# New instruction lists for a fused attention and bilinear feed-forward kernel: the first weight block's first quarter is multiplied first, and 24 identity products stand ahead of it

## The chip, the core and the metric

The kernel runs on one core of one Trainium2 chip. The metric is device microseconds from the first to the last instruction as the runtime times them, lower is better. The core's engines each have a queue of their own that runs in program order: TensorE (PE), VectorE (DVE), ScalarE (ACT), GpSimd (POOL), and SyncE (SP), which here only issues DMA transfers.

## The reference

Eight batches of memory attention, and a feed-forward network with two linear factors on the result:

```python
a = np.exp(phi - phi.max(axis=2, keepdims=True))
a = a / (a.sum(axis=2, keepdims=True) + 1e-09)             # phi: 8 x 8 heads x 576 x 32
k_m = np.einsum('bhsm,bhsd->bhmd', a, k)
v_m = np.einsum('bhsm,bhsd->bhmd', a, v)
scores = (1.0 / np.sqrt(64)) * np.matmul(q, k_m.transpose(0, 1, 3, 2))
attn = softmax(scores)                                     # over 32 memories
x = heads_joined(np.matmul(attn, v_m))                     # 4608 x 512
return ((x @ w1) * (x @ w2) @ w3) @ w_out                  # w1, w2: 512 x 1024; w3: 1024 x 1024; w_out: 1024 x 512
```

The weights come as 64-bit floats, and everything is computed in 32-bit.

## The kernel before, in words

**Weights.** Each weight arrives in HBM as 64-bit words. A block of them is one task of five steps, `C1` to `C5` in the lists: sign (DVE, later ACT), high word (ACT), low word (ACT), shift (DVE), join (DVE). The first task is the first quarter of the first 128 rows of w3 (256 columns), the second is the first 128 rows of w_out, the third is the next quarter of w3's rows; then come further row blocks of w3 and w_out in turn. SP fetches the blocks into a ring of five buffers `raw`, and the last four blocks of w1 and w2 into buffers of the attention.

**The product of w3 and w_out** is made once, in 32-bit products of 128x512 (line 611; each leaves two records in the trace). `X0` and `X1` are the first two products and the next two of row block 0: `X0` needs the first and second task, `X1` the second and third. `W01` to `W07` are the other row blocks of w3's first half, four products each; `W100` to `W171` those of its second half, two products each. What comes out is copied and split into a high and a low part (`K`, `Kh`, `D`, `E`, `Dt`, `Et` and so on), the weight pieces.

**Attention of a batch** has the steps `bm` (PE, maximum spread), `bs` (DVE, maximum added), `be` (ACT, exponent), `mem` (PE, k_m and v_m, lines 254 and 263), `memc` (ACT), `block` (PE, transpose, line 285), `blockc` (ACT, lines 291 and 292, makes `km` and `vm`), `sc0` and `sc1` (PE, scores, line 303), `scc` (DVE, transposes, line 318), softmax steps, and at the end `tr`, `ah`, `al` and for all batches but the first `T1` to `T4`, `Th` and `Tl` (sums of the probabilities, split in high and low).

**Feed-forward of a batch.** `M0` to `M3` (PE, line 420) multiply v_m by w1 and w2. Batch 0 multiplies directly: `A01` is column quarter 0, product 1, and so on (line 718); `a` and `g` take each product out of PSUM on ACT and DVE. The later batches use seven block products `P` (line 748) for eight: `P60` is the sixth block product of quarter 0, which reads the probability sums `Th1` and `Tl1`. Seven products `O` (line 833) multiply the result by the weight pieces; `h` and `l` split their right sides into high and low. `C11` to `C22` copy and store.

**PSUM** has eight banks, kept as four slots on each of two sides; the class `Pair` takes one slot of each. A product waits until the slot that it was given has been read by everyone.

**The order** is written out by hand. Four lists of tokens, `FIRST` (batch 0), `SECOND`, `BATCH` (batches 2 to 6) and `LAST`, say in which order the steps are issued; each engine runs its own steps in that order. A token with "-" is a step of the same batch's attention, "+" of the batch after the next, without a sign of the next. A "!" puts an elementwise step on the other engine: splits and copies (`h`, `Kh`, `r`, `w`, `ah`, `Th`) go from ACT to POOL, differences and products (`l`, `al`, `T`, `Tl`, `v`, `Q`) from DVE to POOL, and `f`, `Sa`, `Sb`, `Sc` from POOL to DVE. Since the lists set which slot, buffer and queue place each step gets, they also set what it waits for.

Ahead of everything, `WARM` identity products of 128x128 run on PE (line 704).

Of the kernel before, what the change touches and what calls it, by code (L numbers as in the profile page):

```python
# [24 lines left out]
FIRST = """
C1 C2 C3 C1 C4 C5 C2 C3 C1 C4 C5 C2 C4 C3 C5 C1 C2 X1 C4 C3 C1 C2 C5 C4 C3 C5 C3 C1 C2 C4 C2 C5 C2 C1 C1 C3 C2 C4 C5
C4 phi0 C3 C1 C3 C4 C5 C1 C2 C3 X0 C5 C1 C2 C4 C5 W01 C3 C1 C4 C2 C3 C2 W02 W03 C4 C5 W04 C5 C1 C3 C1 C4 C5 C1 C2 W05
C4 C3 tok0 kv0 q0 C2 C3 C2 C5 C4 C5 -top -exp W06 -norm C1 C1 C2 C3 C2 C3 W07 -bm C4 C5 K2 Kh2 C4 C5 W101 C1 K3 Kt3
W100 K1 W111 -bs K0 C4 Kt0 Kl2 C3 Kh1 Kh0 W110 C2 r3 C4 -be -mem C5 C3 Kt2 r0 C1 -memc -block C5 -blockc -sc0 -sc1
-scc0 -scc1 Kt1 W121 W120 -mx0 C3 C2 -sb0 W130 -mx1 -ex0 C2 Kl0 -sb1 C3 W131 W141 C4 -sm0 W140 -ex1 C1 C5 C1 W150 W160  # L30
C2 C4 C4 C5 W151 r1! s0 -mu0 -tr0 C3 C2 C1 C1 C2 Kl1 -sm1 C4 C3 C1 W161 Kh3! s3 C4 s1 Kl3 -ah0! -mu1 C3 C5 C5 C2 -M0
-Mh0 -M1 C2 -al0 Q1! C5 W171 -Mh1 -Ml0 W170 A01 -tr1 -ah1! D2 -Ml1 A11 C3 Dt2 C4 Dt3 a01 Dt0 C1 g01 phi1 D3 a11 -al1!
C5 g11 C2 Et2 Et3 C4 A00 a00 g00 C1 -M2 -Mh2 E2 r2! s2 E3 A03 a03 -Ml2 g03 C3 C1 C3 C5 A12 Et0 A23 C4 F0 a12 g12 C5
Q2! A02 F2 t0 w0 tok1 a02 g02 D0 A10 a10 a23 top A13 D1 g23 bm z0 F3 g10 a13 g13 A20 exp bs Q0 a20 A22 g20 t3 be kv1
-M3 w2! y2 norm y0 q1 a22 w3 Dt1 mem E0 t2! z2 -Mh3 memc -Ml3 A32 z3 h10 f0! f1! block Q3 E1 g22 A33 f3! blockc sc0 F1
l10! a32 g32 a33 g33 Et1 h40 h41 scc0 mx0 y3 l41 f2! sc1 M0 Mh0 w1 A21 t1 A31 a31 Ml0 scc1 l40! Sa1! Mr0 a21 g21 mx1
Ms0 g31 A30 a30 g30 Sa3! sb1 z1 sb0 O40 O41 h11 O10 Sa0 h20 l11 O11 h60 Mt0 l20 Sb0 l60 Sc1! y1 Sb3! Sa2 p4 p1 O60
Sc0! O20 Mu0 M1 h21 l21 Sc2 h61 M2 l61 ex0 O21 sm0 O61 ex1 sm1 Sb1! Sb2! h70 l70! h71 mu1 Mr1 mu0 h50 l71 l50! u2 Ms1
C11 tr0 tr1 h51 l51 O70 O71 Mt1 ah0 al0 ah1 Mu1 h30 O50 al1 l30 Mh1 Sc3 h31 q2 T1 Mr2 T3! T2! l31 Ml1 O51 p5 Mh2 C21
O30 C22 T4! Th1 Tl1! O31 Th0 C12 Tl0! Ms2 Mt2! Mu2! Ml2  # L40
"""
SECOND = """
P10 P11 s00 s01 P60 P20 c10 P50 k200 k201 P70 k502 P30 v10 e402 e202 v20 P51 k512 P40 c30 v30 P31 phi1 s10 s11 tok1
h10! l10! P61 k210 P21 top k211 e212 c11 P71 bm v11 e412 exp P12 s20 s21 P41 f0 c31 P22 -M3 bs v21! v41 kv1 v31 be c12
mem -Mr3 norm f3 -Ms3 v12 v40 h11! l11! -Mt3! -Mu3! -Mh3 phi2 P62 memc block k220 k221 +top P52 k522 P72 -Ml3 e422 P32
e222 tok2 P13 blockc sc0 +exp scc0 sc1 scc1 s30 mx2 f2 s31 P42 c32 kv2 +bm v42! f1 P63 k230 k231 v32 P23 P53 k532 sb2
P73 v22! Sa0 P33 Sa1! e432 v43! e232 h60 l60! Sa3 P43 v23 ex2 +bs O10 h20 Sa2 l20 c33 v33 sm2 h70 O11 p1 O60 +be c13
v13 h21 +norm O20 +mem +memc Sb2! Sb1! l21 M0 h61! Sb0 l61 l70 Mr0 O61 Sc0! Mh0 Sb3! O21 h50 mu2 tr2 h71 u2 l71! h51
l51! O70 h41 Ml0 +block +blockc l50 Sc1! O71 O50 ah0 O51 al0 ah1 Ms0 l41 C11 al1! T1 h30 T3 h40 Sc3! l30 l40 M1 p5
Sc2! C22 Mt0 h31! l31! T2! Mh1 q2 Mu0 M2 Mh2 Mr1 Ms1 O30 Mt1 T4! Th0! Ml1 O40 Mu1 Th1 O41 C21 O31 Tl1! Tl0! C12 Mr2  # L50
Ms2 Mt2! Mu2! Ml2
"""
BATCH = """
phi2 P10 -M3 s00 s01 P20 c10 v10 P60 k200 k201 P50 P70 k502 P30 e402 v40! e202 -Mr3 -Ms3 v20! P11 P40 s10 s11 c30 v30
h10! -Mh3 P61 k210 k211 P51 +top -Ml3 -Mt3! P21 k512 P31 c11 e212 +exp -Mu3! P71 +bm P12 e412 P41 f0 v11 s20 s21 c31
P62 sc1 tok2 +bs l10! v31 sc0 v41 kv2 scc0 scc1 k220 h11! P22 P52 v21! c12 v12 mx2 P13 k522 k221 P32 e222 f3 P72 s30
+be P53 s31 P23 k532 P63 c13 e422 v42 k230 k231 v22 f1 l11! sb2 P33 e232 f2 P73 e432 v13 P42 Sa0 ex2 Sa1! P43 +mem v43
c32 v32 Sb0 h20 +norm sm2 +memc M0 Mr0 M2 Sa3 c33 v33 v23! M1 O10 Mh0 Ms0 Ml0 Sb3 O11 Sb1 h21 l21 h50 Sa2! l20! p1 l50
Sb2! h60 l60 O20 O21 Mh1 Sc1! h61 O60 C11 l61 O61 h51 h70 Mt0 Sc0! mu2 Mh2 u2 tr2 ah0 ah1 Sc2! l51! O50 Sc3! l70 h30
h71 l71! O51 p5 Mu0 O70 al0 l30 O30 Ml1 h40 l40 T1 h31 l31 Mr1 Ms1 O71 O31 h41! C22 O40 C12 +block q2 l41! Mt1 +blockc  # L60
T3! O41 Mu1 al1 T2 Th1 C21 Tl1 T4! Th0! Mr2 Tl0! Ms2 Mt2! Mu2! Ml2
"""
LAST = """
Mr1 P10 s00 s01 P11 +bm P20 P60 k200 Ml1 k201 P50 P70 c10 v10 k502 e402 P30 e202 Mr0 T1 +be P40 c30 v20! -M3 v40 s10
s11 P61 v30 h10 -Mh3 -Ml3 phi2 f0 sb2 l10! ah0 P51 k210 kv2 k211 P71 k512 e412 -Mr3 M2 Mu0! -Ms3 -Mt3 P31 e212 P21 tr2
sc1 Mt0 P12 s20 s21 scc1 Ms2 Mh0 v41! v21 P41 c31 v31 Mt2! +block f3! al1 q2 P22 c12 v12 P52 k522 +blockc c11 -Mu3!
P62 k220 k221 T2 P32 Mr2 e222 v11 P53 P72 f1! v22 k532 P13 e422 f2! v42 Sa0 Sa1 P33 +top h11 s30 s31 P63 k230 k231 Mh2
+norm e232 Mu2 P42 Th0! ah1! c32 v32 M1 P73 O10 h60 l60 mx2 T3 Ml0 e432 v43 Sb1 +mem Ms0 sm2 h20 l11! P23 Sb0! O11 p1
v23! Sa2! Tl0 +bs P43 Th1! l20 Sa3! h61 M0 Sb2! +exp O60 c13 v13 O20 l61! O61 h50 l50 Ms1 sc0 c33 v33 tok2 Sb3 h70 l70
h51 O50 l51 h40 h21 al0! l40 Mu1 u2 Sc0! l21 Ml2 Sc2! Sc1! O51 Mh1 p5 h71 Sc3! l71! O70 mu2 O21 C11 O71 C22 Tl1! ex2  # L70
O40 h30! l30! O30 h31 l31 h41! O31 T4! l41 C12 O41 C21 +memc scc0 Mt1!
"""
# [947 lines left out]
```

## Time and profile before

| | before |
|---|---|
| median of 3 runs | 496.7 us (496.6 to 497.26) |
| profiled execution, its own time | 498.98 us |
| its span, first to last instruction | 497.2 us |
| PE busy | 489.2 us (98%) |
| DVE busy | 430.1 us (86%) |
| ACT busy | 338.9 us (68%) |
| POOL busy | 265.2 us (53%) |
| mean granted TensorE clock | 0.997 |

A busy PE is one that has a product under way. The profile's page also cuts the span into slices and gives PE 9 tenths or more in all of them but the first and the last.

### The profile page before, as it was taken

What the parts mean: (1) busy time and instruction counts of PE and PEld (TensorE: products, weight loads), DVE (VectorE), ACT (ScalarE), POOL (GpSimd) and SP (SyncE); (2) the same over time, 40 slices, a digit from 0 to 9 for tenths busy, and PEclk for the clock granted to TensorE, in tenths of its full rate; (3) what the DMA queues carried; (4) which work ended last, traced back from release to release, by engine and by line L of the source; (5) the groups of instructions that cost most, each with busy time, mean ns of one, the idle gap of its engine ahead of it and who ended that gap; (6) DMA issues with size and microseconds to landing.
All of it is one profiled execution on the core that took longest, in us unless ns stands there. A gap on an engine that the chain in (4) does not pass through costs nothing.

```text
span 497.2 us, 11285 instructions
## 1 busy us (share of the span) xinstructions
PE 489.2 (98%) x4312; PEld 421.2 (85%) x4312; DVE 430.1 (86%) x812; ACT 338.9 (68%) x718; POOL 265.2 (53%) x256
## 2 busy tenths in 40 slices
...
GB/s 291 411 412 424 425 117 91 283 2 3 227 298 239 1 98 330 50 2 25 301 154 2 25 231 223 2 25 130 323 3 26 61 107 2 25 49 25 2 1 96
DMA packets 22390, 68.89 MB, mean 139 GB/s; under 512 B 1728, under 2 KB 9920, under 8 KB 20288
## 3 DMA queue, kind: packets, MB, share of 16 engines
...
## 4 chain that ended last, share of the span: by engine, by line
PE 97%; DMA 1%; ACT 0%; DVE 0%; SPq 0%; issue 0%; DVEq 0%
PE ps L833 36%; PE ps L748 32%; PE ps L611 12%; PE ps L420 6%; PE ps L718 5%; PE ps L254 3%; PE ps L303 2%; DMA raw<-in_w3T 1%; PE ps L263 1%; PE ps L285 0%; PE ps L232 0%; SPq L527 0%; DVE wo L599 0%; DVE w L599 0%; ACT w L584 0%
## 5 line engine op out<-in xcount | busy, mean ns | idle before, releaser
L833 PE MATMUL ps<-sh,Wh 128*128 128x288 f32 x448 | 132.8, 296 | 0.0
L833 PE MATMUL ps<-sh,Wl 128*128 128x288 f32 x448 | 132.2, 295 | 0.0
L833 PE MATMUL ps<-sl,Wh 128*128 128x288 f32 x448 | 132.0, 295 | 0.0
L818 POOL TENSOR_TENSOR sl<-g,sh 128x576 fp32r<-128x576 f32 x43 | 65.4, 1523 | 72.7 <-ACT sh L501 48.8
L833 PEld LDWEIGHTS ps<-sh,Wh 128*128 128x128 f32 x448 | 84.2, 188 | 6.8 <-ACT mh L431 5.0
L833 PEld LDWEIGHTS ps<-sh,Wl 128*128 128x128 f32 x448 | 84.2, 188 | 0.0
L833 PEld LDWEIGHTS ps<-sl,Wh 128*128 128x128 f32 x448 | 84.2, 188 | 0.0
L501 ACT CAST sh<-g 128x576 fp32r<-128x576 f32 x78 | 52.3, 684 | 24.3 <-PE ps L833 14.5
L611 PE MATMUL ps<-wo,w 128*128 128x512 f32 x128 | 57.5, 608 | 2.4 <-DVE w L599 2.4
L767 ACT COPY c<-ps 128x288 f32<-128x288 f32 x112 | 41.6, 412 | 18.9 <-PE ps L748 16.7
L773 DVE TENSOR_TENSOR c<-ps,c 128x288 f32<-128x288 f32 x112 | 44.8, 451 | 10.4 <-ACT c L767 8.4
L611 PEld LDWEIGHTS ps<-wo,w 128*128 128x128 f32 x128 | 24.6, 195 | 33.6 <-issue 29.3
L748 PE MATMUL ps<-sh,ms 128*128 128x288 f32 x224 | 51.8, 296 | 0.0
L728 ACT COPY a_sb<-ps 128x288 f32<-128x288 f32 x72 | 29.0, 406 | 22.7 <-PE ps L748 19.8
L818 DVE TENSOR_TENSOR sl<-g,sh 128x576 fp32r<-128x576 f32 x55 | 43.2, 792 | 0.7 <-ACT sh L501 0.4
L438 DVE TENSOR_TENSOR ml<-ps,mh 128x512 fp32r<-128x512 f32 x64 | 40.9, 681 | 1.3 <-ACT mh L431 1.2
L748 PEld LDWEIGHTS ps<-sh,ms 128*128 128x128 f32 x224 | 38.2, 188 | 1.0 <-ACT ps L761 0.8
L732 DVE TENSOR_TENSOR g<-ps,a_sb 128x288 f32<-128x288 f32 x72 | 32.0, 448 | 6.2 <-ACT a_sb L728 4.9
L456 DVE TENSOR_TENSOR tmp<-ps,tmp 128x256 f32<-128x256 f32 x84 | 32.8, 419 | 4.4 <-ACT mh L431 2.1
L431 ACT CAST mh<-ps 128x512 fp32r<-128x512 f32 x64 | 34.4, 596 | 2.2 <-PE ps L420 1.1
L748 PE MATMUL ps<-ah,mh 128*128 128x288 f32 x112 | 34.6, 309 | 0.0
L748 PE MATMUL ps<-sh,mh 128*128 128x288 f32 x112 | 33.2, 296 | 0.0
(151 smaller groups left out, 1280.4 us busy)
## 6 DMA issues: line engine op xcount, KB each, us to landing
...
q<-in_qT SPq DMA_DIRECT2D x8, 1152.0 KB, 5.9
...
```

What stands on the lines that cost most here:

```text
L420: nc.tensor.matmul(ps[t][g * M : (g + 1) * M], lhsT=vm[b % 2][d, g], rhs=w12_sb[q][d, :, g], start=True, stop=True,)
L431: nc.scalar.copy(out=mh[:, t], in_=ms["ps", q][t].rearrange("p (w f) -> p w f", w=2))
L438: nc.vector.tensor_tensor(out=ml[:, t], in0=x, in1=ms[q][0][:, t].bitcast(F32), op=ALU.subtract)
L456: nc.vector.tensor_tensor(out=tmp[:, j], in0=x, in1=tmp[:, y], op=op)
L501: nc.scalar.copy(out=out, in_=in_)
L611: nc.tensor.matmul(pw[r, i // 2][i % 2][:, cols], lhsT=x[:, i * P : (i + 1) * P], rhs=wos[k // half][:, k % half, cols], start=k == 0 and ...
L732: engine.tensor_tensor(out=G[n, f // half][:, f % half], in0=b, in1=a, op=ALU.mult)
L748: nc.tensor.matmul(G[bank, q][w][:, :HALF], lhsT=xs[x][:, w], rhs=ys[y], start=i in (1, 5) and k == 0, stop=i in (2, 3, 4) and k == 2, ski ...
L767: nc.scalar.copy(out=G["kept", i, q][:, j], in_=x)
L773: nc.vector.tensor_tensor(out=c, in0=x, in1=c, op=ALU.add)
L818: flexible().tensor_tensor(out=lo, in0=src, in1=hi.bitcast(F32), op=ALU.subtract)
L833: nc.tensor.matmul(ps[j][:, :HALF], lhsT=piece(x, s, 2 * part + k)[:, jc], rhs=y[:, k], start=i in first and part == 0 and k == 0 and t == ...
```

## The change

All four lists are new, `WARM` is 24 instead of 16, and `block_product` looks up the sums of the weights only for the products that use them, so that a list may name a product before the sums exist. No computation is added but the eight identity products; no step is left out. The core of the diff (of the lists the first line of each of two):

```diff
-WARM = 16
+WARM = 24
 FIRST = """
-C1 C2 C3 C1 C4 C5 C2 C3 C1 C4 C5 C2 C4 C3 C5 C1 C2 X1 C4 C3 C1 C2 C5 C4 C3 C5 C3 C1 C2 C4 C2 C5 C2 C1 C1 C3 C2 C4 C5
+C1 C2 C3 C1 C2 C4 C4 C3 C5 C5 X0 C1 C2 C3 C4 C5 C1 C2 C4 C3 C1 C2 C4 C3 C5 C5 C3 C1 X1 C2 C4 C2 C4 C2 C1 C5 C1 C3 C5
...
 BATCH = """
-phi2 P10 -M3 s00 s01 P20 c10 v10 P60 k200 k201 P50 P70 k502 P30 e402 v40! e202 -Mr3 -Ms3 v20! P11 P40 s10 s11 c30 v30
+P10 s00 s01 -M3 phi2 P60 tok2 P20 P50 c10 v10 k200 k201 k502 P70 e402 v40! P30 e202 P11 +top -Mr3 -Ms3 s10 s11 P40 c30
...
     def block_product(b, i, q, G):
-        (mh, ml), (sh, sl) = ready["M", b][q], ready["M", b]["sums", q]
+        of = ready["M", b]
         t, u = {1: (0, 0), 2: (1, 0), 4: (1, 1), 7: (0, 1), 5: (None, 0), 6: (None, 1), 3: (None, 2)}[i]
-        xs = [m[:, t, :, u * P : (u + 1) * P] for m in (mh, ml)] if t is not None else [m[:, u] for m in (sh, sl)]
+        xs = [m[:, t, :, u * P : (u + 1) * P] for m in of[q]] if t is not None else [m[:, u] for m in of["sums", q]]
```

**First place: DVE's queue at the very start.** `L569` is a task's sign, `L594` its shift, `L599` (ISA) its join; 128x256 are the quarters of w3, 128x512 the rows of w_out. Before:

```order
L569 TENSOR_SCALAR uw<-raw 128x256 [waits DMAHW0_49]
L569 TENSOR_SCALAR u<-raw 128x512 [waits DMAHW1_49]
L594 TENSOR_SCALAR w_131<-w_131 128x256 [waits Activation_49]
L599 ISA w_131<-w_131,uw 128x512 [waits DVE_49,Activation_49]
L569 TENSOR_SCALAR uw<-raw 128x256 [waits DMAHW2_49,DVE_49]
L594 TENSOR_SCALAR wo_83<-wo_83 128x512 [waits Activation_49]
L599 ISA wo_83<-wo_83,u 128x1024 [waits DVE_49,Activation_49]
```

With the change:

```order
L569 TENSOR_SCALAR uw<-raw 128x256 [waits DMAHW0_49]
L569 TENSOR_SCALAR u<-raw 128x512 [waits DMAHW1_49]
L594 TENSOR_SCALAR w_139<-w_139 128x256 [waits Activation_49]
L594 TENSOR_SCALAR wo_83<-wo_83 128x512 [waits Activation_49]
L599 ISA w_139<-w_139,uw 128x512 [waits DVE_49]
L599 ISA wo_83<-wo_83,u 128x1024 [waits DVE_49,Activation_49]
L569 TENSOR_SCALAR uw<-raw 128x256 [waits DMAHW2_49,DVE_49]
```

The shift and the join of w_out's first rows no longer stand behind the sign of the third task, which waits for its transfer. On PE `X0` comes ahead of `X1`; before, `X1` came first.

**Second place: PE from the spread maximum to the scores of batch 0, and SP's queue ahead of it.** In PE's rows L232 is `bm`, L611 a run of products of w3 and w_out, L254 and L263 are `mem`, L285 is `block`, L303 the scores. Before:

```order
L232 MATMUL ps<-ident,mx 128x128 x2
L611 MATMUL ps<-wo_83,w_277 128x512 x8
L254 MATMUL ps<-kv_267,a 32x128 x8
L254 MATMUL ps<-kv_265,a 32x128 x8
L254 MATMUL ps<-kv_267,a 32x128 x8
L254 MATMUL ps<-kv_265,a 32x128 x8
L263 MATMUL ps<-kv_269,a 32x128 x8
L285 MATMUL ps<-ident,kvm 128x128 x2
L303 MATMUL ps<-q,km_71 32x288 x16
```

With the change:

```order
L232 MATMUL ps<-ident,mx 128x128 x2
L611 MATMUL ps<-wo_83,w_288 128x512 x4
L254 MATMUL ps<-kv_261,a 32x128 x8
L254 MATMUL ps<-kv_259,a 32x128 x8
L254 MATMUL ps<-kv_261,a 32x128 x8
L254 MATMUL ps<-kv_259,a 32x128 x8
L263 MATMUL ps<-kv_263,a 32x128 x8
L611 MATMUL ps<-wo_83,w_288 128x512 x2
L285 MATMUL ps<-ident,kvm 128x128 x2
L611 MATMUL ps<-wo_83,w_288 128x512 x2
L303 MATMUL ps<-q,km_71 32x288 x16
```

Of the eight products between `bm` and `mem` four now stand behind `mem`, two on either side of `block`. SP's transfers, before and then with the change (L170 is phi, L175 its other layout `a`, L183 and L190 k and v, L195 q):

```order
L170 DMA ph<-in_phiT 128x1152
L527 DMA raw<-in_w3T 128x2x1024 x4
L175 DMA a<-in_phi_tok 128x1152
L183 DMA kv_265<-in_kv 128x2x1024
L183 DMA kv_267<-in_kv 128x2x1024
L190 DMA kv_269<-in_kv 128x512
L195 DMA q<-in_qT 128x2304
```

```order
L527 DMA raw<-in_w3T 128x2x1024 x3
L170 DMA ph<-in_phiT 128x1152
L175 DMA a<-in_phi_tok 128x1152
L183 DMA kv_259<-in_kv 128x2x1024
L183 DMA kv_261<-in_kv 128x2x1024
L190 DMA kv_263<-in_kv 128x512
L527 DMA raw<-in_w3T 128x2x1024
L195 DMA q<-in_qT 128x2304
```

The last block of w3 moved from ahead of k and v to between v and q; q has the same bytes ahead of it as before.

**Third place: POOL at the end of batch 2, a run of `BATCH`.** L384 are `T` steps, L818 is an `l`, L499 a copy, L395 a `Tl`. Before:

```order
L384 TENSOR_TENSOR at<-at 128x288 [waits DVE_49] x2
L499 CAST sh<-at 128x576 [waits PE_49,Activation_49,Pool_49]
L395 TENSOR_TENSOR sl<-at,sh 128x576 [waits PE_49,Pool_49]
L499 CAST ms<-tmp 128x768 [waits DVE_49]
L466 TENSOR_TENSOR ms<-tmp,ms 128x768 [waits Pool_49]
```

With the change:

```order
L384 TENSOR_TENSOR at<-at 128x288 [waits DVE_49]
L818 TENSOR_TENSOR sl<-g_2307,sh 128x576 [waits PE_49,Activation_49]
L384 TENSOR_TENSOR at<-at 128x288 [waits Pool_49]
L395 TENSOR_TENSOR sl<-at,sh 128x576 [waits PE_49,Activation_49] x2
L499 CAST ms<-tmp 128x768 [waits DVE_49]
```

Both `Tl` steps are now on POOL (`Tl1` was on DVE), and on PE `P60`, which reads what `Tl1` writes, stands directly behind `M3`, where `P20` stood between them before.

## Rows read from the trace of the kernel before

**Rows 1.** The page: span, and busy time of PE.
```profile
span 497.2 us, 11285 instructions
...
PE 489.2 (98%) x4312; PEld 421.2 (85%) x4312; DVE 430.1 (86%) x812; ACT 338.9 (68%) x718; POOL 265.2 (53%) x256
```

**Rows 2.** Who PE waited for: us in total, times, longest us.
```profile
PE ps L611 <- DVE w L599: 2.4, 1, 2.4
...
PE ps L285 <- ACT kvm L276: 0.5, 1, 0.5
PE ps L303 <- ACT km L291: 0.4, 1, 0.4
```

**Rows 3.** The chain that ended last, in time order: start us, us, what.
```profile
10.10 29.34 PE ps L611 x64
...
46.53 1.89 PE ps L254 x64
...
50.27 1.66 PE ps L303 x31
...
80.58 9.71 PE ps L718 x72
```

**Rows 4.** Windows: us, busy us of each engine, granted clock, DMA share, GB/s.
```profile
10.00:11.00 1.00, 0.90 (x1) 0.50 (x2) 1.00 (x5) 1.00 (x3) 0.00 (x0) 0.50 1.00 410
...
13.00:14.00 1.00, 1.00 (x4) 0.39 (x3) 0.96 (x3) 0.58 (x1) 0.00 (x0) 0.81 1.03 414
```

**Rows 5.** Timeline of PE, the last identity products, in two windows.
```profile
6.71 0.94 PE L704 MATMUL ps<-ident 128*128 128x128 f32 x7
...
7.05 0.61 PE L704 MATMUL ps<-ident 128*128 128x128 f32 x4
```

**Rows 6.** Timeline of ACT and DVE: steps of w_out's first and last rows.
```profile
6.18 0.79 ACT L590 ACTIVATE u<-raw 128x512 uint16<-128x512 uint32 x1
...
8.59 0.69 DVE L599 CUSTOM_DVE_ANT_0 wo<-wo,u 128x1024 uint16<-128x1024 uint16 x1
...
29.16 1.22 DVE L599 CUSTOM_DVE_ANT_0 wo<-wo,uw 128x2048 uint16<-128x2048 uint16 x1
```

**Rows 7.** SP's issues, landing times from issue (last number), and a window's rate.
```profile
27.50 2.25 SPq L190 DMA_DIRECT2D kv<-in_kv  x1
29.79 0.43 SPq L195 DMA_DIRECT2D q<-in_qT  x1
...
q<-in_qT SPq DMA_DIRECT2D x1, 1152.0 KB, 17.5
...
kv<-in_kv SPq DMA_DIRECT2D x1, 256.0 KB, 17.0
...
30.00:40.00 10.00, 10.00 (x27) 4.45 (x26) 7.75 (x12) 8.33 (x12) 0.00 (x0) 1.00 1.02 414
```

**Rows 8.** Timeline of DVE: two joins, and the steps around product A03.
```profile
44.91 1.75 DVE L599 CUSTOM_DVE_ANT_0 w<-w,u 128x2048 uint16<-128x2048 uint16 x1
...
58.40 1.22 DVE L599 CUSTOM_DVE_ANT_0 w<-w,u 128x2048 uint16<-128x2048 uint16 x1
...
79.15 0.74 DVE L681 TENSOR_TENSOR c<-ps,sl 128x256 f32<-128x256 f32 x2
79.82 0.68 DVE L594 TENSOR_SCALAR w<-w 128x1024 int32<-128x1024 int32 x1
80.42 0.44 DVE L732 TENSOR_TENSOR g<-ps,a_sb 128x288 f32<-128x288 f32 x1
80.78 1.27 DVE L635 TENSOR_TENSOR Wl<-ps,Wh 128x512 fp32r<-128x512 f32 x2
```

**Rows 9.** Around the head of batch 3: DVE, POOL, and the chain.
```profile
292.82 1.07 DVE L395 TENSOR_TENSOR sl<-at,sh 128x576 fp32r<-128x576 f32 x1 [1.15 <-ACT sh L501]
...
293.37 1.83 POOL L395 TENSOR_TENSOR sl<-at,sh 128x576 fp32r<-128x576 f32 x1
...
293.56 1.02 PE ps L420 x16
```

More of the change, by code (lines that the diff above doesn't have):

```diff
@@ L23 @@
 ORDERED = {EngineType.SP, EngineType.PE, EngineType.Activation, EngineType.DVE, EngineType.Pool}
-WARM = 16
+WARM = 24
 FIRST = """
-C1 C2 C3 C1 C4 C5 C2 C3 C1 C4 C5 C2 C4 C3 C5 C1 C2 X1 C4 C3 C1 C2 C5 C4 C3 C5 C3 C1 C2 C4 C2 C5 C2 C1 C1 C3 C2 C4 C5
-C4 phi0 C3 C1 C3 C4 C5 C1 C2 C3 X0 C5 C1 C2 C4 C5 W01 C3 C1 C4 C2 C3 C2 W02 W03 C4 C5 W04 C5 C1 C3 C1 C4 C5 C1 C2 W05
-C4 C3 tok0 kv0 q0 C2 C3 C2 C5 C4 C5 -top -exp W06 -norm C1 C1 C2 C3 C2 C3 W07 -bm C4 C5 K2 Kh2 C4 C5 W101 C1 K3 Kt3
-W100 K1 W111 -bs K0 C4 Kt0 Kl2 C3 Kh1 Kh0 W110 C2 r3 C4 -be -mem C5 C3 Kt2 r0 C1 -memc -block C5 -blockc -sc0 -sc1
@@ L30 @@
[L30 to L39, printed above, removed]
@@ L40 @@
-O30 C22 T4! Th1 Tl1! O31 Th0 C12 Tl0! Ms2 Mt2! Mu2! Ml2
+C1 C2 C3 C1 C2 C4 C4 C3 C5 C5 X0 C1 C2 C3 C4 C5 C1 C2 C4 C3 C1 C2 C4 C3 C5 C5 C3 C1 X1 C2 C4 C2 C4 C2 C1 C5 C1 C3 C5
+C2 C4 C3 W01 C1 C5 C3 C1 C2 C4 C4 C5 C3 C5 C1 C2 C4 W02 C3 C1 C2 C4 C5 C3 W03 C2 C1 C3 phi0 C4 C5 C5 tok0 W04 kv0 C1
+C1 C2 C3 W05 C4 q0 C5 C2 C4 C3 C5 C2 C1 C4 C1 C2 C3 C4 W06 C5 C2 C3 C4 W07 K0 K1 Kt0 -top Kh0! -exp -bm -bs W100 K2
+Kt1 Kh2! K3 Kt3 -norm W101 -be r0! C1 C5 -mem C3 C5 W110 -memc -block Kh3! s0 W111 C2 C3 C4 -blockc -sc0 -sc1 Kh1 W121
@@ new lines @@
+C1 C3 C5 -scc0 -scc1 W120 -mx0 Kl0 C2 -mx1 -sb0 -ex0 C2 C3 W131 W141 W151 Kt2 W130 r2 r1! W161 Kl1 C1 r3! s3 -sb1 -sm0
+W140 C4 -ex1 C4 C5 W171 -mu0 C1 C5 C2 C4 C3 C2 C4 W150 W160 C1 C1 C2 -tr0 -sm1 C5 Kl2 -M0 -ah0! -mu1 C4 C3 C1 C3 -al0
+C2 C5 C2 C5 C4 C4 -Mh0 -Ml0 Dt2 -M1 Q1! -Mh1 -Ml1 W170 C3 F2 A01 a01 C1 C2 A11 -tr1 s2 Dt3 g01 Dt0 C5 -ah1! -al1! A00
+a11 g11 D2 E2 -M2 Q2! D3 a00 E3 phi1 C4 Et3 g00 Et2 C1 -Mh2 -Ml2 A03 F3 C3 C1 tok1 A12 a12 top C3 g12 A02 C5 a02 a03
+g02 w2 F0 Kl3 g03 Et0 C5 D1 t2! A13 a13 g13 A10 s1 a10 D0 E0 kv1 y2 Q0! exp bm g10 bs f2 t0 z0 A22 a22 A23 w0 A20 a23
```

54 lines of the change are left out of this document (30 added, 24 removed).

## The prediction

> **What bounds the kernel now.** I read the busy times first. PE is busy for 489.2 of 497.2 us [rows 1], so a new order can win only in the 8 us in which it isn't, or where PE is busy and slow. The list of what PE waited for shows the first: 2.4 us for the join of a w3 block, and in the whole rest of the run two waits, 0.5 us for `memc` and 0.4 us for `blockc` of batch 0 [rows 2]. From 10.10 us on the chain is PE's own work [rows 3]. The windows show the second: PE stood still from 7.65 us, where its last identity product ends [rows 5], to 10.10 us, and from 10.0 us on the granted clock is 0.50, the 1.2 GHz level. It is 0.81 over the window from 13 to 14 us [rows 4], which is 0.50 for 0.38 us and full speed after that, so PE worked for 3.3 us at half speed and lost 1.65 us. Past 14 us the clock costs nothing. So there are 2.4 + 1.65 + 0.9 us to win at the start, and everything behind batch 0 can only stay or get worse.
>
> **The change part by part.**
>
> *The start.* In the trace the join of w_out's first rows starts at 8.59 us, though their last ACT step ends at 6.97 us [rows 6], because DVE's queue has a sign ahead of it that waits for the third task's transfer. With that sign behind the join, the join follows the ACT step: it takes 0.69 us [rows 6], so `X0` has its data at about 7.7 us. It doesn't start then, since 8 more identity products stand ahead. Each leaves two records; the last ones start 0.113 us apart (three starts between 6.71 and 7.05 us) [rows 5]. 16 x 0.113 = 1.8 us, so PE comes to `X0` at 7.65 + 1.8 = 9.45, say 9.4 us, without standing still. That is 0.7 us earlier than 10.10. And as PE doesn't stand still, I expect the clock to stay at its upper level: the 1.65 us are saved too. Bounds: 16 records at the mean of all, 0.2 us, would end at 10.8 us and cost 1.4 us more; the 1.65 us are saved or not.
>
> *Data for the last row blocks.* 64 records took 29.34 us [rows 3], less 1.65 us that is 0.433 each. `X0` to `W05` are 48 records, 20.8 us, so PE comes to `W06` at 30.2 us. That product needs the join that ends at 29.16 + 1.22 = 30.38 us [rows 6]; its place among the joins is the same and it hangs on a transfer, so it doesn't move. PE waits 0.2 us. (If the start goes worse by 0.2 us, this wait goes away, so small errors at the start cost less than they seem.) `W07` ends at 30.4 + 6.9 = 37.3, `bm` and four products at 0.2 + 3.5 later: 41.0 us.
>
> *`mem` of batch 0.* It started at 46.53 us [rows 3] and needs v and k. The last piece of them lands at 27.50 + 17.0 = 44.5 us [rows 7]. One block of w3, 1 MB, moves behind it; at 414 GB/s [rows 7] that is 2.5 us, so 42.0 us, and the piece ahead of it (0.63 us of bytes) 41.3 us. PE waits 0.3 us. `mem` and the four products around `block` take PE to 41.3 + 2.3 + 1.75 + 0.2 + 1.75 = 47.3 us, and they hide `memc` and `blockc`: the 0.5 and 0.4 us go. The scores need q, which has the same bytes ahead of it as before and lands at 29.79 + 17.5 = 47.3 us [rows 7], and `blockc`, which ACT does behind two steps of the moved block. I take 0.2 us of waiting (bounds 0 and 0.5). They end at 49.2 us, and ended at 50.27 + 1.66 = 51.93 [rows 3]: 2.7 us gained.
>
> *DVE in batch 0.* From the scores' transposes on DVE hardly rests, and sets when PSUM slots come free. Product `A03` starts at 80.58 us [rows 3]; the slot of its second half, 0.8 us later, comes free with a `g` that ends at 80.42 + 0.44 = 80.86 [rows 8]: 0.5 us to spare. With the change that slot comes free with `Et3`, and behind the transposes DVE's queue has more up to there: one shift (0.68 us), and `E2`, `E3` (1.27) and `Et3` (0.37) in place of two `Et` (0.74) and the `g` (0.44) [rows 8], 0.5 us net. 0.68 + 0.5 - 0.5 leaves 0.7 us. The bounds are 0 (the moved shift and join find a gap) and 1.2 us (no slack). I take 0.6 us: ten steps later the new list has less on DVE, not more, as `Q0` and two `f` go to POOL. Those moved steps I cost at nothing on POOL, which is busy for 265.2 us [rows 1].
>
> *Batches 1 to 7.* PE waits for nothing here, the number of products is the same, so the gain is 0. The new places of `v`, `S`, `l` and `T` steps are covered by PE's products; what it costs if not is a rival below.
>
> *Sum.* 0.7 + 1.65 + 0.9 = 3.25 us gained, 0.2 + 0.3 + 0.2 + 0.6 = 1.3 us given back, 2.0 us net. The profiled execution takes 498.98 us, 1.8 us more than its span, and the sum gives it 497.0 us. The median of the plain runs is 2.3 us below the profiled one; less 2.0 us it becomes 494.7 us.
>
> **The rivals.** (0.2%, 1 us, is about what a measurement of this kernel can tell from no change.)
>
> *The gain is eaten by DVE and POOL in batch 0.* POOL gets more between 37 and 50 us (copies `Kh`, `r`) and between 70 and 95 us (`Q0`, `f`). A join of the same size took 1.22 us at 58.40 us with POOL idle, and 1.75 us at 44.91 us with POOL at work [rows 8]. Three or four joins and shifts that are stretched by 0.3 to 0.5 us in the tight stretch before `A03` cost 1 to 2 us. For it: DVE has 0.5 us to spare there. Against it: DVE's own work is what goes to POOL. It leaves 0.3 to 1.0 us of gain: 496.0 us. The Trainium skill (page "SBUF — State Buffer", section "SBUF: two separate sides") says that DVE and GpSimd share a pair of ports that one instruction holds as an exclusive lock until it ends, so that the other blocks; the trace agrees in those two joins, and by that rule work moved to POOL gives DVE less than its length, which speaks for this rival.
>
> *The head of each batch waits; slower.* At the end of a `BATCH` run `Tl1` goes from DVE (1.07 us) to POOL (its neighbour took 1.83 us there), behind a `T` and an `l`, and `P60`, which reads it, moves up to directly behind `M3`, which ends at 293.56 + 1.02 = 294.58 us [rows 9]. In the times of before, a `Tl1` on POOL from 292.82 us on would end at 294.65, just too late. What is queued behind `P60` is all of PE. For it: `Tl0` follows on POOL and `P50` needs it 1.6 us later. Against it: the `T` steps stand earlier in DVE's and POOL's queues, ahead of `C21` and `Ms2`, so `Tl1` should start earlier by 1 us or more. Five batch heads (3 to 7) have it; from 0.4 us each it eats the 2.0 us, and with 0.8 us each (one POOL step late) the kernel is slower by 2.0 us: 498.7 us.
>
> *The change doesn't do what it says at the start.* The extra products end at 10.8 us (the bound above): then `X0` has no gain of its own, `W06` is reached at 31.6 us, and the net gain is 0.9 us: 495.8 us. For it: PE ran its first identity products at a wider step than the last. Against it: the last seven are steady.
>
> **How the numbers follow.** The forecast, 493.4 (nothing given back) to 495.5 us, has a chance of 0.66; DVE and POOL eat most of it 0.19; the start falls short 0.05; batch heads wait 0.10. Faster by over 0.2% (below 495.7 us) is the forecast's case and a part of the two small gains: 0.70. Within 0.2% is the rest of those two and a little of the batch heads: 0.20; slower 0.10. The range is 493.4 to 497.0 us: it leaves out the batch heads at their full price, and the end of the first rival that no row supports.
>
> **What would show it.** In the profile after, the first product of line 611 should start between 9.3 and 9.6 us with a granted clock of 1.00 from 10 to 14 us; `mem` (line 254) at 41 to 42 us; the first scores (line 303) at 47 to 48 us; `A01` some 2.6 us and `A03` some 2.0 us ahead of before. In PE's list of waits there should be no wait for `kvm` and `km` above 0.3 us, and small ones for DVE near 77 to 80 us. I am wrong if the clock falls to 0.50 anyway, if PE waits above 1 us for DVE or POOL between 60 and 110 us, or if waits for `Tl` recur every 52 us behind line 420.

## The result, and the profile after

The changed kernel takes 502.1 us (median of 4 runs, 501.77 to 503.41); the kernel before took 496.71 us beside it. The ratio is 1.0107, with a 95% interval of 1.0091 to 1.0123: slower by 1.1%, where 0.4% faster was forecast. The profiled execution takes 501.86 us.

The page of after, against [rows 1]:

```profile
span 500.1 us, 11271 instructions
...
PE 489.9 (98%) x4328; PEld 420.7 (84%) x4328; DVE 431.1 (86%) x793; ACT 346.8 (69%) x732; POOL 260.8 (52%) x261
```

The shares of busy time are those of before. What moved is in the list of whom PE waited for (us in total, times, longest us), which answers to [rows 2]:

```profile
PE ps L833 <- DVE sl L818: 1.7, 1, 1.7
PE ps L704 <- POOL ident masks.py:199: 1.4, 1, 1.4
PE ps L748 <- DVE g L732: 1.3, 1, 1.3
PE ps L833 <- ACT c L856: 0.7, 1, 0.7
PE ps L833 <- ACT c L869: 0.5, 1, 0.5
PE ps L611 <- DVE wo L599: 0.3, 1, 0.3
PE ps L254 <- DVE c L773: 0.3, 1, 0.3
PE ps L748 <- POOL g L732: 0.2, 1, 0.2
PE ps L833 <- DVE c L773: 0.2, 1, 0.2
```

The waits of [rows 2] are gone or small: 2.4 us for the first join is none, `kvm` and `km` are none. New are 2.9 us behind line 833 (the products `O` of batch 0) and 1.3 us behind line 748 (a block product of batch 3). These are the two largest places where the changed kernel loses.

The chain of after up to the scores of batch 0, against [rows 3] (start us, us, what):

```profile
30.29 7.13 PE ps L611 x16
...
41.08 1.93 PE ps L254 x64
...
47.24 1.13 PE ps L303 x32
```

`mem` starts at 41.08 and the scores at 47.24 us. The forecast had 41.3 and 47.3.

**What the kernel before usually does.** A second profile of the kernel before (experiment 1) has a span of 495.0 us, not 497.2. Its windows, against [rows 4], and its chain:

```profile
10.00:11.00 1.00, 1.00 (x4) 0.46 (x3) 1.00 (x3) 1.00 (x2) 0.00 (x0) 1.00 1.04 426
13.00:14.00 1.00, 1.00 (x4) 0.46 (x3) 1.00 (x3) 0.41 (x2) 0.00 (x0) 1.00 1.09 406
```

```profile
9.52 27.73 PE ps L611 x64
...
48.08 1.66 PE ps L303 x31
```

The granted clock (third from the end) is 1.00, the 2.4 GHz level, where the first profile had 0.50, though PE stood still for 2.4 us ahead of 9.52 us here as well; the 64 records take 27.73 us, not 29.34; and the join that they wait for comes 0.6 us earlier. By the scores this execution is 2.2 us ahead of the one that the prediction read, about the distance of that one (498.98 us) to the median. Executions like the one that the prediction read recur: of 78 more of the kernel before, nine show a mean granted clock of 0.995 to 0.997 and take 498.4 to 499.1 us, 68 show 0.999 or 1.00 and take 496.4 to 497.5 us (one took 776.75 us at 0.579). Where in those nine the clock fell is not known.

So the change is measured against this second profile. The table takes starts from PE's timeline (scores: line 303; heads of batches: the first record of line 748), of the second profile of either kernel (spans 495.0 and 500.2 us):

| stretch | before, us | after, us | difference |
|---|---|---|---|
| start to the scores of batch 1 | 98.41 | 97.03 | -1.4 |
| from there to the head of batch 1 | 31.16 | 34.87 | +3.7 |
| batch 1 (list `SECOND`) | 55.72 | 56.99 | +1.3 |
| batch 2 | 52.57 | 52.51 | -0.1 |
| batch 3 | 52.56 | 54.16 | +1.6 |
| batches 4 to 6 | 155.08 | 154.95 | -0.1 |
| batch 7 to the last product | 46.14 | 46.34 | +0.2 |

The sum is 5.2 us, the difference of the spans, and near the 5.4 us of the medians. Of the 1.4 us at the start, 0.9 are won by the scores of batch 0, and 0.5 in the scores themselves, which take 1.13 us instead of 1.66.

**The 3.7 us.** In and just ahead of this stretch the new `FIRST` sends `l20`, `l60` and `l71` from DVE to POOL and `l40` the other way, and of the S steps five from POOL to DVE and one back. From 98.38 us on the chain of after leaves PE and runs over DVE. DVE's timeline there (start us, us, line, operation, xcount), and under it POOL's:

```profile
107.47 2.43 DVE L802 TENSOR_TENSOR g<-g,g 128x288 f32<-128x288 f32 x3
109.82 0.45 DVE L732 TENSOR_TENSOR g<-ps,a_sb 128x288 f32<-128x288 f32 x1
110.19 0.74 DVE L344 TENSOR_REDUCE st<-s_sb 128x18 f32<-128x576 f32 x1
...
114.64 1.69 DVE L804 TENSOR_TENSOR g<-g,g 128x288 f32<-128x288 f32 x1
...
118.09 1.56 DVE L804 TENSOR_TENSOR g<-g,g 128x288 f32<-128x288 f32 x1
119.58 2.17 DVE L466 TENSOR_TENSOR ms<-tmp,ms 128x768 fp32r<-128x768 f32 x1
```

```profile
107.97 3.21 POOL L818 TENSOR_TENSOR sl<-g,sh 128x576 fp32r<-128x576 f32 x2 [5.36 <-DVE g L802]
114.31 1.70 POOL L818 TENSOR_TENSOR sl<-g,sh 128x576 fp32r<-128x576 f32 x1 [3.13 <-ACT sh L501]
117.91 3.02 POOL L818 TENSOR_TENSOR sl<-g,sh 128x576 fp32r<-128x576 f32 x2 [1.90 <-DVE st L345]
```

The same kind of DVE steps in the second profile of before, and under them the next POOL step, ahead of which POOL is idle for 7.04 us:

```profile
110.87 0.45 DVE L804 TENSOR_TENSOR g<-g,g 128x288 f32<-128x288 f32 x1
111.24 0.45 DVE L802 TENSOR_TENSOR g<-g,g 128x288 f32<-128x288 f32 x1
111.61 0.45 DVE L804 TENSOR_TENSOR g<-g,g 128x288 f32<-128x288 f32 x1
111.98 0.95 DVE L466 TENSOR_TENSOR ms<-tmp,ms 128x768 fp32r<-128x768 f32 x1
```

```profile
114.09 0.84 POOL L804 TENSOR_TENSOR g<-g,g 128x288 f32<-128x288 f32 x1 [7.04 <-DVE sl L818]
```

Lines 802 and 804 are S steps, 0.45 us each elsewhere in the trace of after too, and line 466 takes 0.95. Where one starts behind a POOL step `l` (line 818) that is still running, it is longer by 1.2 us, as if it had stood until that was through: line 804 ends at 116.33 us, 0.3 us behind POOL's step of 114.31, and line 466 at 121.75, 0.8 us behind the last of POOL's two. Four meetings make 4.9 us, on an engine that is busy for 33.6 of the 34 us from 98 to 132. Line 732, with one input in PSUM, and line 344, a reduction, run beside the same POOL steps at their usual length.

The Trainium skill (page "SBUF — State Buffer", sections "SBUF: two separate sides" and "Who interferes with whom") draws this line: a `tensor_tensor` with both inputs in SBUF contends with a GpSimd instruction that reads SBUF, the one that starts first holds the shared ports to its end, and `tensor_reduce` never does. The trace agrees in all of these rows. It also shows that the order of the starts decides who stands. From 95 us on, line 466 meets a POOL `tensor_tensor` six times in it. The five times that DVE started first it takes 0.95 us and POOL's step (line 395) 1.82 us instead of 1.43; the one time that POOL did, line 466 takes the 2.17 us shown above.

### The profile page after: what moved, and what is told of

It reads as the page before. It is cut to its first block, busy times and chain, and to the rows that moved or that the text cites. A ratio compares the mean times of both kernels' runs of the same rounds, so it can differ in the third digit from the quotient of the medians.

```text
span 500.1 us, 11271 instructions
## 1 busy us (share of the span) xinstructions
PE 489.9 (98%) x4328; PEld 420.7 (84%) x4328; DVE 431.1 (86%) x793; ACT 346.8 (69%) x732; POOL 260.8 (52%) x261
## 4 chain that ended last, share of the span: by engine, by line
PE 82%; DVE 9%; DMA 5%; issue 1%; ACT 1%; SPq 1%; POOL 0%; DVEq 0%; ACTq 0%
PE ps L833 31%; PE ps L748 28%; PE ps L611 7%; PE ps L420 5%; PE ps L718 4%; PE ps L254 3%; DMA raw<-in_w_out 2%; PE ps L303 2%; DMA raw<-in_w3T 2%; DMA ph<-in_phiT 1%; DVE sl L818 1%; DVE tmp L456 1%; DVE g L804 1%; SPq L527 1%; DVE c L773 1%
## 5 line engine op out<-in xcount | busy, mean ns | idle before, releaser
L818 POOL TENSOR_TENSOR sl<-g,sh 128x576 fp32r<-128x576 f32 x47 | 68.5, 1463 | 83.9 <-ACT sh L501 76.5
L501 ACT CAST sh<-g 128x576 fp32r<-128x576 f32 x90 | 60.6, 691 | 12.2 <-PE ps L833 8.5
L611 PE MATMUL ps<-wo,w 128*128 128x512 f32 x128 | 57.1, 598 | 0.5 <-DVE wo L599 0.3
L748 PE MATMUL ps<-sh,ms 128*128 128x288 f32 x224 | 52.9, 299 | 1.5 <-DVE g L732 1.3
L611 PEld LDWEIGHTS ps<-wo,w 128*128 128x128 f32 x128 | 23.6, 190 | 30.9 <-issue 25.9
L732 POOL TENSOR_TENSOR g<-c 128x288 f32<-128x288 f32 x42 | 33.7, 806 | 24.9 <-DVE c L773 24.7
L818 DVE TENSOR_TENSOR sl<-g,sh 128x576 fp32r<-128x576 f32 x51 | 41.7, 831 | 1.4 <-POOL sh L499 1.1
```

What stands on the lines that cost most here:

```text
L501: nc.scalar.copy(out=out, in_=in_)
L611: nc.tensor.matmul(pw[r, i // 2][i % 2][:, cols], lhsT=x[:, i * P : (i + 1) * P], rhs=wos[k // half][:, k % half, cols], start=k == 0 and ...
L748: nc.tensor.matmul(G[bank, q][w][:, :HALF], lhsT=xs[x][:, w], rhs=ys[y], start=i in (1, 5) and k == 0, stop=i in (2, 3, 4) and k == 2, ski ...
L818: flexible().tensor_tensor(out=lo, in0=src, in1=hi.bitcast(F32), op=ALU.subtract)
```

## The experiments

Theory A: the start gains what the second profile leaves to gain, 1.4 us, and POOL's `l` steps that meet DVE's in batch 0 lose 3.7 us. The rivals: the lists of the later batches lose it (theory B); DVE's own queue is too long, whatever POOL does.

**1. The kernel before once more**, with no edit.

> The kernel before, unchanged, profiled a second time. Theory A (the 1.65 us at half clock and a join that came 0.5 us later were of that one profiled execution, not of the kernel; so there was nothing to win there): granted clock 1.00 from 10 to 14 us, first product of row blocks at 9.6 us, scores of batch 0 at 48.2 us, first block product of batch 1 at 129.7 us, span near 495 us. The rival (before always pays it): 0.50 from 10 to 13 us, 131.8 us, span 497 us.

Measured: 496.86 us, span 495.0; clock 1.00, first product at 9.52, scores at 48.08, head of batch 1 at 129.57 us. Theory A, in all numbers. That the granted clock fell to 0.50 was a matter of that execution, not of the usual one.

**2. 24 identity products and nothing else.**

```diff
-WARM = 16
+WARM = 24
```

> The kernel before, with 24 identity products and nothing else. Its first product waits for DVE's join at 9.6 us; the added products end at 9.0 to 9.6 us. Theory A (no clock drop in most runs of before, so nothing to win): 496.7 us, within 0.3. The prediction's step (PE that doesn't stand still keeps its clock: 1.65 us): 495.0 us.

Measured: 496.77 us, ratio 0.9994 (0.9982 to 1.0006). The wait for the join shrinks from 2.4 to 0.2 us, since identity products stand in it, and nothing else moves: scores at 48.03 us. So the 1.65 us that the prediction gave to the clock are not there to win in the usual execution. Whether the added products spare an execution that would have lost clock is not shown: none of the 10 here shows a mean granted clock below 0.999, but two of the eight of the changed kernel, which has them too, show 0.993 and 0.996.

**3. The new `FIRST` alone, and 4. the new later lists alone.** In 3 the lists of batches 1 to 7 are set back (below the first line of one), in 4 `FIRST` and `WARM`.

```diff
 SECOND = """
-P10 s00 P11 s01 P60 phi1 P20 c10 v10 k200 k201 P50 k502 tok1 P70 e402 P30 e202 v40! s10 P40 top s11 P61 P51 c30 bm P21
+P10 P11 s00 s01 P60 P20 c10 P50 k200 k201 P70 k502 P30 v10 e402 e202 v20 P51 k512 P40 c30 v30 P31 phi1 s10 s11 tok1
...
```

> FIRST and the 24 identity products are new, the lists of batches 1 to 7 are those of before. Theory A (the gain of 3.5 us is there until 98 us and is lost between 98 and 132 us of batch 0, where DVE's S steps run beside POOL's l steps and are stretched): the first block product of batch 1 starts at 132 us as before, and the time is that of before, 496.7 us, within 0.8 us. Theory B (the lists of the later batches hold the loss): 493 to 494 us.

> FIRST and the 16 identity products are those of before, the lists of batches 1 to 7 are new. Theory A: only what batch 1 loses (1.2 us) and, in some runs, a phi transfer that comes late for DVE's maximum (1.4 us in the profiled run): 497.9 to 499.5 us. Theory B: the whole loss and no gain, 500 to 502.5 us.

Measured: 3 takes 501.13 us, ratio 1.0084 (1.0056 to 1.0113). It was wrong as a time for theory A, because that still counted 3.5 us of gain at the start; the loss of 34.87 us where 31.16 is due is there in full. Its profiled execution, 499.88 us, is the fastest of its four; the other three take 501.0 to 502.82 us at mean granted clocks of 0.993 to 0.997, so the median holds more than what the list loses. 4 takes 498.09 us, ratio 1.0023 (1.0011 to 1.0036): the later lists hold 1.3 us, all of it in batch 1 in its trace (57.02 us). Theory B falls.

**5. POOL's five `l` steps out of the way.**

```diff
         lo = G["X", i, part][1] = big.tile([P, 2, HALF], F32R, name="sl", tag="sl", bufs=4)
+        if by_act:
+            nc.scalar.copy(out=lo, in_=src)
+            return
...
+                by_act = b == 0 and what in ("l20!", "l60!", "l70!", "l71!", "l50!")
```

> The changed kernel, with l20, l60, l70, l71 and l50 of batch 0 left out of POOL: ScalarE writes a copy in their place, so that part of the low halves is not computed. DVE's list is not touched. Theory A (POOL's l steps stretch DVE's S steps): DVE's lines 802, 804 and 466 between 107 and 122 us go back to 0.45 and 0.95 us each, and the first block product of batch 1 starts at 128.5 to 130 us; the time is 499 to 500 us. The rival (DVE's own queue): these steps keep their lengths of 0.8 to 2.2 us, 132 us and 502 us.

Measured: 497.67 us, ratio 1.0010 (0.9999 to 1.0021), 4.4 us less than the change, with DVE's list as it was. That is below the expected 499 to 500 us, and 1.6 us of it are luck: in this trace the transfer of phi came early and batch 3 took 52.5 us (see 13). The head of batch 1 is at 129.73 us, 32.3 us behind the scores where the change has 34.87 and before 31.16. DVE's rows (one line was added ahead, so that line 802 is 803 here):

```profile
107.82 1.19 DVE L803 TENSOR_TENSOR g<-g,g 128x288 f32<-128x288 f32 x3
...
113.67 0.45 DVE L805 TENSOR_TENSOR g<-g,g 128x288 f32<-128x288 f32 x1
...
115.89 0.40 DVE L805 TENSOR_TENSOR g<-g,g 128x288 f32<-128x288 f32 x1
116.20 0.95 DVE L467 TENSOR_TENSOR ms<-tmp,ms 128x768 fp32r<-128x768 f32 x1
```

The steps have their usual lengths. What stretched them was POOL's work, not their own queue. It gives back 2.5 of the 3.7 us; the other 1.2 us stay open. PE's one wait there is:

```profile
PE ps L837 <- ACT c L860: 0.9, 1, 0.9
```

ACT works without a break from 120.08 us to this copy, with two of the copies that the experiment added in it (1.4 us), so this wait may be of its own making; the change has a wait of 0.7 us at the same line (856 there).

**6. Ten marks of batch 0 as before, the order of the change.** One of the lines:

```diff
-Sa0! h11 z1 O40 sb0 sb1 l41 Sa3! l11 z3 Sb3! ex0 Sa2! ex1 O10 Mh0 h20 Sb0! Sa1 Sb1! Sb2! O11 O41 g30 sm1 h60 l60! l20!
+Sa0 h11 z1 O40 sb0 sb1 l41 Sa3! l11 z3 Sb3! ex0 Sa2 ex1 O10 Mh0 h20 Sb0 Sa1! Sb1! Sb2! O11 O41 g30 sm1 h60 l60 l20
...
```

> The changed kernel, with ten marks in batch 0 as before: Sa0, Sa2, Sb0, Sc2, Sc3 on POOL and Sa1 on DVE, l20, l60, l71 on DVE and l40 on POOL; the order is that of the change. Theory A: no S step of DVE above 0.6 us between 98 and 126 us, the first block product of batch 1 at 129 to 130 us instead of 132.1, the time 499 to 500 us. A rival (DVE's queue is simply too long there, whatever POOL does; its work is about the same in both, 5 steps of 0.45 us out, 1 of 0.45 and a net of two l steps in): 501.5 to 502.5 us.

Measured: 501.1 us, ratio 1.0082 (1.0063 to 1.0102); 35.37 us from the scores of batch 1 to its head, more than the change. A miss. The two `l` steps that stay on POOL, and an S step between them, met other DVE steps:

```profile
116.87 1.98 DVE L350 TENSOR_TENSOR s_sb<-s_sb,st 128x576 f32<-128x576 f32 x1
...
119.55 1.39 DVE L345 TENSOR_SCALAR st<-st 128x18 f32<-128x18 f32 x1
```

```profile
116.30 1.93 POOL L818 TENSOR_TENSOR sl<-g,sh 128x576 fp32r<-128x576 f32 x1 [0.34 <-ACT sh L501]
118.20 1.32 POOL L804 TENSOR_TENSOR g<-g,g 128x288 f32<-128x288 f32 x1
119.49 1.42 POOL L818 TENSOR_TENSOR sl<-g,sh 128x576 fp32r<-128x576 f32 x1
```

Line 350 is 0.75 us and line 345 0.18 us where POOL is idle. So it is not these ten marks as such: an S step of POOL costs too where it meets such a step of DVE in this stretch, and the order decides which meet. Line 345 is a `tensor_scalar` from SBUF to SBUF, so the steps with two inputs in SBUF are not the only ones that stand.

**7. Three marks in the kernel before.** `l20`, `l60` and `l71` of batch 0 go to POOL; no token moves.

```diff
-Ms0 g31 A30 a30 g30 Sa3! sb1 z1 sb0 O40 O41 h11 O10 Sa0 h20 l11 O11 h60 Mt0 l20 Sb0 l60 Sc1! y1 Sb3! Sa2 p4 p1 O60
-Sc0! O20 Mu0 M1 h21 l21 Sc2 h61 M2 l61 ex0 O21 sm0 O61 ex1 sm1 Sb1! Sb2! h70 l70! h71 mu1 Mr1 mu0 h50 l71 l50! u2 Ms1
+Ms0 g31 A30 a30 g30 Sa3! sb1 z1 sb0 O40 O41 h11 O10 Sa0 h20 l11 O11 h60 Mt0 l20! Sb0 l60! Sc1! y1 Sb3! Sa2 p4 p1 O60
+Sc0! O20 Mu0 M1 h21 l21 Sc2 h61 M2 l61 ex0 O21 sm0 O61 ex1 sm1 Sb1! Sb2! h70 l70! h71 mu1 Mr1 mu0 h50 l71! l50! u2 Ms1
```

> The kernel before, with three marks more: l20, l60 and l71 of batch 0 go from DVE to POOL; no other token moves. DVE has 3 times 0.75 us less work of its own. Theory A (a POOL l step that reads two buffers in SBUF locks out a DVE step that does so too, for up to 1.2 us each): DVE steps of lines 802, 804 or 466 at 1.5 us and more beside them, the first block product of batch 1 at 130 to 131.5 us instead of 129.6, the time 497.2 to 499 us. The rival (work that leaves DVE is simply won, or covered): 496.7 us or less, and no DVE step of these lines above 0.6 and 1.0 us.

Measured: 501.13 us, ratio 1.0095 (1.0081 to 1.0109). DVE was relieved of 2.25 us, and the head of batch 1 comes at 133.81 us, 4.2 us later: the right sign, and more than double the size. PE's waits in the stretch are 0.9 us for ACT, 0.5 us for DVE, and 1.3 us for POOL itself (lines 635 and 818). The steps that POOL had before came later behind these three, and met further steps of DVE, as these rows of DVE and then of POOL show:

```profile
118.54 1.39 DVE L345 TENSOR_SCALAR st<-st 128x18 f32<-128x18 f32 x1
...
122.21 2.65 DVE L350 TENSOR_TENSOR s_sb<-s_sb,st 128x576 f32<-128x576 f32 x2
```

```profile
118.48 2.81 POOL L818 TENSOR_TENSOR sl<-g,sh 128x576 fp32r<-128x576 f32 x2
122.80 1.45 POOL L818 TENSOR_TENSOR sl<-g,sh 128x576 fp32r<-128x576 f32 x1 [1.51 <-ACT sh L501]
```

**8. The same three marks set back in the change.**

```diff
-Sa0! h11 z1 O40 sb0 sb1 l41 Sa3! l11 z3 Sb3! ex0 Sa2! ex1 O10 Mh0 h20 Sb0! Sa1 Sb1! Sb2! O11 O41 g30 sm1 h60 l60! l20!
+Sa0! h11 z1 O40 sb0 sb1 l41 Sa3! l11 z3 Sb3! ex0 Sa2! ex1 O10 Mh0 h20 Sb0! Sa1 Sb1! Sb2! O11 O41 g30 sm1 h60 l60 l20
...
-l71! C11 l50! mu0 tr0 tr1 M2 Mh2 O71 O50 Ms1 Mt1 l30 ah0 h31 q2 l51 O51 ah1 Mu1 al0 al1 T1 T3! T2! Mh1 T4! l31 C21 Ml1
+l71 C11 l50! mu0 tr0 tr1 M2 Mh2 O71 O50 Ms1 Mt1 l30 ah0 h31 q2 l51 O51 ah1 Mu1 al0 al1 T1 T3! T2! Mh1 T4! l31 C21 Ml1
```

> The changed kernel, with l20, l60 and l71 of batch 0 on DVE (three marks); S steps as in the change. POOL keeps l70 and l50 there. Theory A, with the l steps as the main offenders: 3 of the 5 meetings go, 3.6 us less stretch against 3 times 0.75 us more of DVE's own work: the first block product of batch 1 1 to 2 us earlier, 500 to 501 us. If any POOL step would do: within 0.5 us of 502.1 us.

Measured: 500.7 us, ratio 1.0075 (1.0056 to 1.0095); 33.61 us from scores to head, 1.3 us less than the change and 2.4 more than before. As expected of the `l` steps (3.6 us less stretch against 2.25 us more work of DVE), and it is only a third of the loss. What makes up the other 2.4 us in this order is not shown.

**9, 10 and 11. The new start with the old order behind it.** The new `FIRST` runs up to a token, and what is left of batch 0 follows in the order and with the marks of before; so do the lists behind it. The token is `-sc1` (9), `A01` (10) and `-Ml3` (11). Of 11, the first line that differs from the change:

```diff
-g23 be f0! Dt1 g22 -M3 -Mh3 Et1 -Ml3 norm a20 h40 h10 Q3 mem y0 z2 l40 A32 t3 memc block a32 g32 f1 w3 y3 g20 F1
+g23 be f0! Dt1 g22 -M3 -Mh3 Et1 -Ml3 a20 g20 t3 norm y0 q1 w3 mem z2 memc A32 z3 h10 f1! block Q3 E1 A33 f3! blockc
...
```

> 24 identity products and the new FIRST up to sc1 of batch 0's scores; from there on the steps of before in their order, with their marks; the lists of batches 1 to 7 of before. Theory A: the start is worth 0.9 to 1.5 us of scores, and what follows is as before: 495.2 to 496.2 us. The prediction's own size of the start (2.7 us): 494.0 us. A rival (DVE has no room to follow a PE that comes earlier): 496.8 us, with waits of PE for DVE between 60 and 132 us.

> As m1_start_only, with the new FIRST up to product A01 (71 us) and the steps of before from there on. Theory A: 495.2 to 496.2 us. If the order between the scores and A01 were what hurts: above 497 us.

> As m1_start_only, with the new FIRST up to Ml3 (some 92 us) and the steps of before from there on: the stretch from 98 to 132 us has the order and marks of before. Theory A (the loss is in the S and l steps of that stretch): 495.2 to 496.5 us. If the loss has its root ahead of it (steps that DVE or POOL owe from 70 to 92 us): 499 to 501 us, with the block products of batch 1 from 132 us on.

Measured: 496.11 (ratio 0.9991, 0.9982 to 1.0001), 496.5 (0.9996, 0.9986 to 1.0006) and 496.13 us (0.9986, 0.9977 to 0.9995). From the scores of batch 1 to its head 31.16, 31.67 and 31.27 us: with the old order there, the 3.7 us are gone, whichever list led up to it. At the head of batch 1 they are 0.6 to 1.2 us ahead of before; the medians show 0.2 to 0.6 of it, and only the interval of 11 leaves out no change. PE's waits in 11:

```profile
PE ps L704 <- POOL ident masks.py:199: 1.4, 1, 1.4
PE ps L254 <- DMA kv<-in_kv: 0.2, 1, 0.2
```

**12. 11 with the new `BATCH` and `LAST`**, the old `SECOND`.

```diff
 BATCH = """
-phi2 P10 -M3 s00 s01 P20 c10 v10 P60 k200 k201 P50 P70 k502 P30 e402 v40! e202 -Mr3 -Ms3 v20! P11 P40 s10 s11 c30 v30
+P10 s00 s01 -M3 phi2 P60 tok2 P20 P50 c10 v10 k200 k201 k502 P70 e402 v40! P30 e202 P11 +top -Mr3 -Ms3 s10 s11 P40 c30
...
```

> m3_to_Ml3 with the new BATCH and LAST and the old SECOND. From the periods of x2_rest_only (52.51 instead of 52.57 us each, and 0.12 us at the end) 0.3 to 0.4 us less than m3_to_Ml3: 495.7 us. The rival (the early step for the maximum of phi waits for its transfer in some batches): 496.5 us and more.

Measured: 497.08 us, ratio 1.0009 (0.9996 to 1.0021), the time that the rival had. Batch 3 takes 54.0 us.

**13. The change once more**, with no edit.

> The changed kernel, unchanged, profiled and timed again: 501.8 to 502.5 us. Theory A: 3.5 to 3.8 us are lost between the first scores of batch 1 and its first block product as in the first profile. Open is the 1.4 us that batch 3 lost there to a late phi transfer: if it is chance, batch 3 takes 52.5 us this time.

Measured: 502.14 us, ratio 1.0118 (1.0099 to 1.0138); 34.87 us from scores to head again. And batch 3 is slow again, by 1.6 us, so this is not chance. Its chain:

```profile
242.98 6.60 DMA ph<-in_phiT
...
249.60 1.35 DVE mx L214
...
252.08 0.38 DVE g L732
```

DVE's maximum of phi (`+top`) stands early in the new `BATCH`, and waits for its transfer; a product of batch 3 (`v30`, line 732) that frees a PSUM slot stands behind it, and PE behind that. With the old `BATCH` the transfer at this place is long too (5.9 us in the second profile of before), but there DVE comes to this step 1.1 us after the transfer has landed.

**14 and 15. That step later**, in the change and in 12.

```diff
-P10 s00 s01 -M3 phi2 P60 tok2 P20 P50 c10 v10 k200 k201 k502 P70 e402 v40! P30 e202 P11 +top -Mr3 -Ms3 s10 s11 P40 c30
-P61 k210 k211 v30 -Mh3 P21 c11 P51 k512 P71 -Ml3 +exp e412 P31 e212 f1 +bm P12 P41 s20 s21 c31 P62 v11 +bs -Mt3! -Mu3!
+P10 s00 s01 -M3 phi2 P60 tok2 P20 P50 c10 v10 k200 k201 k502 P70 e402 v40! P30 e202 P11 -Mr3 -Ms3 s10 s11 P40 c30
+P61 k210 k211 v30 -Mh3 P21 c11 P51 k512 +top P71 -Ml3 +exp e412 P31 e212 f1 +bm P12 P41 s20 s21 c31 P62 v11 +bs -Mt3! -Mu3!
```

> The changed kernel, with the maximum of phi in BATCH (the token for the batch after the next) behind v30 and the copies of P51 instead of right behind P11. Theory A (DVE's queue stands still for the phi transfer and holds v30's product behind it): batch 3 takes 52.5 us instead of 54.1, nothing else changes: 500.4 to 500.9 us. The rival (something else in batch 3): 502.1 us.

> m5_mix with the same token moved: batch 3 at 52.5 us, 495.4 to 495.9 us, which would be below both kernels. The rival: 497.1 us as m5_mix.

Measured: 14 takes 500.93 us (ratio 1.0097, 1.0063 to 1.0132), at the end of what theory A expected, with batch 3 at 52.50 us though the transfer took 5.6 us. 15 takes 495.43 us, ratio 0.9970 (0.9959 to 0.9980): faster than both kernels, by 1.3 us against before. (In its trace the transfer took 4.7 us, so it is 14 that shows what the moved token does.) It is the start of the change, the order of before from `-Ml3` to the end of batch 1, and the later lists of the change with one token moved.

## Why the prediction was wrong

- **The chip's clock and the first product, 0.7 + 1.65 us: wrong.** 2.2 us of what was to be won were a loss of the one profiled execution, which the prediction itself put 2.3 us above the median without asking what they were; it took its sum off the median, in which they don't stand. The kernel's usual start is that of experiment 1. The other terms at the start held: `mem` at 41.08 us against 41.3, scores at 47.24 against 47.3 (they end at 48.37, not 49.2, since they take 1.13 us), the 0.9 us of `kvm` and `km` won, and the remark that errors there cost little: in the second profile of after the first product comes at 9.57 instead of 8.48 us and `mem` at the same time. Measured, the start is worth 1.4 us.
- **"Those moved steps I cost at nothing on POOL": the step that failed.** The prediction says so of `Q0` and two `f`, with POOL's busy time as the reason, and for the stretch from the scores of batch 1 to its head, where three `l` go to POOL, it has no term at all. That stretch became 3.7 us longer. 2.5 us of this go with the five `l` steps of POOL (experiment 5), all of it with the order and marks of before (9 to 11), and three of the marks alone cost 4.2 us in the kernel before (7); 1.2 us stay open between the new order and a copy on ACT. POOL's share of busy time says nothing about such a price, as most of it falls on DVE's steps. The prediction asked for this in its first rival, with the right mechanism and rows, and lost it twice: it put the place before `A03`, where after loses nothing, and set the price at 1 to 2 us, no more than the gain. The argument against that rival, that DVE's own work is what goes to POOL, does not hold in experiment 7: 2.25 us of work off DVE cost 4.2 us.
- **The 0.6 us before `A03`: not there.** From `A01` to `A03` PE takes the same time in either kernel (5.78 us in the chains).
- **"Batches 1 to 7 ... the gain is 0": wrong by 2.9 us.** Batch 1 loses 1.3 us. PE's list of waits names 0.5 us of it, 0.2 us for a `v` on POOL and 0.3 us of line 254 behind DVE's line 773; the rest was not settled. Batch 3 loses 1.6 us at a step for which no rival was named: a wait for a transfer at the head of DVE's queue (experiments 13 and 14).
- **The rival of the batch heads: it didn't happen.** `P60` doesn't wait for `Tl1` in any batch of after, and batches 4 to 6 take no longer than before.

With what was measured in place of the wrong steps the sum is 1.4 us gained and 3.7, 1.3 and 1.6 us lost: 5.2 us slower.
